# Idle products on a constant zero, a shorter table chain, an earlier load of one head's queries, one head's keys rounded on ScalarE, and the last two stores issued by ScalarE

## The chip, the cores and the metric

The kernel runs on one core of a Trainium2 chip. The metric is the device time of one execution in microseconds. Three runs of the kernel before took 411.08, 411.6 and 412.46 us; their median is 411.6 us. The engines are called by their short names: PE is TensorE (products), PEld its weight loads, DVE is VectorE, ACT is ScalarE, POOL is GpSimd and SP is SyncE, which here only issues transfers. A trailing q (SPq, ACTq, PEldq) means the sequencer that feeds the engine.

## The reference, cut to what matters

Three blocks in a row, all in float32. First an attention of 2 batches and 8 heads over 768 positions of 64 channels, in which each position sees the first `n_global` (8) positions and the last `n_local` (96), with a distance penalty for each head; then a block that rotates its input by learned angles and mixes it over positions and channels; then a gated block with a convolution over three positions.

```python
scores = scale * np.matmul(q, k.transpose(0, 1, 3, 2))
rel = pos[:, None] - pos[None, :]
is_global = pos[None, :] < int(n_global)
is_local = (rel >= 0) & (rel < int(n_local))
dist = np.where(is_global & ~is_local, float(n_local), np.abs(rel))
scores = scores - slopes[:, None, None] * dist[None, :, :]
scores = np.where(is_global | is_local, scores, -1e9)
a = softmax(scores); attn = np.matmul(a, v)
...
theta = x @ w_theta; zr, zi = x * np.cos(theta), x * np.sin(theta)
y = np.einsum('ts,bsd->btd', w_tok_r, zr) + np.einsum('ts,bsd->btd', w_tok_i, zi)
u = x + y; x = u + np.maximum(u @ w_ch, 0.0)
...
h = np.maximum(x @ w_in, 0.0)
out = (h * sigmoid(conv3(h, conv_w))) @ w_out
```

The large products are made of float32 numbers split into a rounded high part and the rest, three products for one, so that PE can run them in its faster rounded format.

## The kernel before, in words

`begin` runs ahead of everything. It loads the four words of `n_global` and `n_local` (L1036, on ACT's queue), the keys of heads 0 and 1 (`pairs`, L1038, on SP's queue) and the queries of head 0 (L1041, on ACT's queue). It lets PE make idle products whose results nobody reads (L1043 and L1044): they multiply `scratch[D:P]`, 64 partitions that DVE has just filled with zeros (L1042), by themselves. POOL writes the distances into `R` (L1051 to L1054). DVE turns the words into the floats `ng` and `nl` (L1063 to L1067), makes the flag `fi` that says whether the fast path holds (L1071 to L1073), and builds `table`, the masked distance of each of 232 columns, with a second form `X` of its last 128 columns for the first row of tiles (L1074 to L1079).

`build` then reads `fi` into a register of each engine (L1023) and branches (L1026). `arm` opens the pools of the fast path, and `run_fast` does the work. Its order is written out by hand: one loop over `j`, three steps for each of 16 heads (i = j // 3), and in a step the scores of step j, the softmax of j - 1 (DVE, L377), the exponentials of j - 2 (ACT, L386), the transposes of j - 3 (PE, L395), their copy out of PSUM for j - 4 (ACT, L82) and the product with V for j - 5 (PE). Each engine executes its instructions in this order, and the code of the steps sets it.

Heads 0 to 7 (`WHOLE`) use unrounded queries and keys, two heads to one tile of keys. A query of an even head fills the upper 64 partitions of its tile `whole[i % 4]` and the lower 64 are zero, an odd one the other way. `query` loads one (L329), `pair` two with their keys (L334). Heads 8 to 15 use split numbers: `load` brings queries (L254) and the keys' lower half (L255) into a stage by SP's queue, `keys` brings the keys a second time into the final tile by POOL's queue, which rounds them on the way (L260), and `split` makes the rest: ACT rounds the scaled queries (L304), DVE makes the queries' low part (L308) and the keys' low part (L90 with the form 64x816, input `qk`). Between these, `net.run` converts weights that arrive as 64 bit floats (L98 on ACT, L102, L106, L110 and L90 on DVE). From head 9 on, products `TH<-wth,xTs` of the second block are placed between those of the heads.

`tables` makes the scaled penalty of a head on POOL, for head 0 on DVE (L341). `Mix.tail` follows with the rest of the network, and `ff_out` ends it: each of 12 tiles of the output is copied from PSUM and stored by SP's queue (L700), the last tile in two halves, the first copied by ACT and the second by DVE. After the last store every engine branches to the end of the program, where SP waits for the transfers' semaphores and all engines meet.

Of the kernel before, what the change touches and what calls it, by code (L numbers as in the profile page):

```python
# [12 lines left out]
F32 = mybir.dt.float32  # L13
F32R = mybir.dt.float32r
I32 = mybir.dt.int32
AF = mybir.ActivationFunctionType
ALU = mybir.AluOpType
AX = mybir.AxisListType

B, H, S, D = 2, 8, 768, 64  # L20
DM, DFF = H * D, 1024
P = 128
NT = S // P
KC = DM // P
NF = DFF // P
NH = B * H
NG = 8
NPREV = 96
# [8 lines left out]
STAGE = S + NT * KW  # L37
BIG = float(2.0 ** 40)
# [2 lines left out]
TURN = 6.283185  # L41
TWO32 = float(2.0 ** 32)
WHOLE = range(8)
LAG_SM, LAG_EXP, LAG_T, LAG_EV, LAG_PV, LAG_N = 1, 2, 3, 4, 5, 6


REBIAS = 2.0 ** -112
QSCALE = -0.125


class Net:
# [173 lines left out]
class Attention:  # L225
# [21 lines left out]
    def load(self, i, whole=False):  # L247
        if whole or (i < NH and i not in WHOLE):
            b, h = divmod(i, H)
            src, st = self.net.io["qk"][b, :, h, :], self.st[i % 2]  # L250
            if whole:
                self.nc.sync.dma_start(st, src)
            else:
                self.nc.sync.dma_start(st[:, 0:S], src[:, 0:S])  # L254
                self.nc.sync.dma_start(st[D:P, S:STAGE], src[D:P, S:STAGE])  # L255

    def keys(self, i):
        if i < NH and i not in WHOLE:
            b, h = divmod(i, H)
            self.nc.gpsimd.dma_start(self.K(i), self.net.io["qk"][b, :, h, S:STAGE])  # L260

# [49 lines left out]
class FastAttention(Attention):  # L311
# [3 lines left out]
    def __init__(self, net, xs):  # L315
        super().__init__(net, xs)
        self.state = {}
        self.o = {}
        x, y = net.head["scratch"], xs[1].rearrange("p t d -> p (t d)")
        self.whole = [x[:, 0:S], y[:, 0:S], y[:, STAGE : STAGE + S], x[:, STAGE : STAGE + S]]  # L320
        self.both = [x[:, S:STAGE], y[:, S:STAGE]]

    def half(self, i):
# [12 lines left out]

    def tables(self, i):

        e = self.nc.gpsimd if i else self.nc.vector
        x = 2.0 ** -(i % H + 1) / (QSCALE if i in WHOLE else 1.0)  # L340
        e.tensor_scalar(self.bias[i % 2], self.net.head["table"], x, None, op0=ALU.mult)  # L341

    def chunks(self, tp):
        return [(u, a) for u in range(2) for a in range(2) if 2 * tp + u > 0 or a == 1]
# [4 lines left out]
    def scores(self, j):  # L349
# [4 lines left out]
        sp = net.bank("TH", 1) if tp == 2 and i < NH // 2 + 2 else net.bank("S", 2)  # L354
        if i in WHOLE:
            Q, K = self.whole[i % 4].unsqueeze(1), self.both[i // 2 % 2]
# [11 lines left out]
    def softmax(self, j):  # L368
        net, s = self.net, self.state[j]
        s["nm"] = net.small.tile([P, 2], F32, tag="nm", name=net.uid("nm"), bufs=3)  # L370
        i, tp = divmod(j, 3)
        bias = self.bias[i % 2].bitcast(F32)
        for u in range(2):
            c, t = slice(RW * u, RW * u + RW), bias[:, 0:RW]
            if tp + u == 0:
                c, t = slice(PG, RW), bias[:, RW:]
            self.nc.vector.tensor_tensor_reduce(  # L377
                self.sS[tp][:, c], s["sp"][:, c], t, scale=QSCALE if i in WHOLE else 1.0, scalar=3.0e38,
                op0=ALU.add, op1=ALU.min, accum_out=s["nm"][:, u : u + 1],
            )  # L380
# [84 lines left out]
class Mix:  # L465
# [223 lines left out]
    def ff_out(self, b, t, bank, e, c=slice(0, DM)):  # L689
        n = self.net  # L690
        k = 0
        for f in range(NF):
            g, w = self.g[b][f], self.wout[f]
            tc = slice(P * t, P * t + P)
            for a, x in ((0, 0), (1, 0), (0, 1)):
                n.mm(bank[:, c], g[:, a, tc], w[:, x, c], k == 0, k == 3 * NF - 1)
                k += 1
        o = n.tmp()
        n.hi(e, o[:, c], bank[:, c])
        self.nc.sync.dma_start(n.io["out"][b, P * t : P * t + P, c], o[:, c])  # L700

    def tail(self, early):

# [160 lines left out]
def run_fast(tc, net):  # L864
    nc, io = net.nc, net.io
    xs = [net.slot(f"xs{b}", [P, NT, DM], F32, "xs") for b in range(2)]
    att = FastAttention(net, xs)
    mix = Mix(net, xs)
    att.tables(0)
    att.query(1)  # L870
    nc.scalar.activation(att.whole[1][0:D], net.head["half_pi"][0:D].to_broadcast([D, S]), AF.Copy, scale=0.0)
    att.tables(1)
    nc.gpsimd.memset(att.whole[2][D:P], 0.0)
    att.load_v(0)
# [33 lines left out]
    for j in range(NJ + LAG_N + 3):  # L908
        i, tp = divmod(j, 3)
# [22 lines left out]
                att.keys(i + 2)  # L932
        if i > 0 and i + 1 not in WHOLE:
            if tp == 0:
                att.split(i + 1, "  A")
            elif tp == 1:
                att.split(i + 1, "   V")
                att.split(i + 1, " V")
# [15 lines left out]
        if splits and (splits[0][0] == 0 or theta0 == "done"):  # L954
            b, c = splits.popleft()
# [76 lines left out]
def begin(nc, io, net, small, head, idle):  # L1032

    w = small.tile([P, 4], I32, name="words")
    scratch = small.tile([P, 2584], F32, name="scratch")
    nc.scalar.dma_start(w, io["n"].bitcast(I32).rearrange("(o n) -> o n", o=1).to_broadcast([P, 4]))  # L1036
    for x in (slice(0, 2 * KW), slice(2 * KW, NT * KW)):
        nc.sync.dma_start(scratch[:, S:STAGE][:, x], io["pairs"][0, :, x])  # L1038
    qc = (slice(0, 2 * P), slice(2 * P, S))
    for x in qc:  # L1040
        nc.scalar.dma_start(scratch[0:D, x], io["qk"][0, 0:D, 0, x])  # L1041
    nc.vector.memset(scratch[D:P, 0:S], 0.0)  # L1042
    for x in (512, 512, 256):  # L1043
        net.mm(idle[:, 0:x], scratch[D:P, 0:P], scratch[D:P, 0:x], True, True)  # L1044
    nc.vector.memset(scratch[0:D, STAGE : STAGE + S], 0.0)

    R = scratch[:, STAGE + S : STAGE + S + RW]
    table = small.tile([P, RW + P], F32, name="table")
    T, X = table[:, 0:RW], table[:, RW:]
    V, G, O = slice(0, NPREV), slice(NPREV, PG), slice(PG, RW)  # L1050
    nc.gpsimd.iota(R[:, V], pattern=[[-1, NPREV]], base=NPREV, channel_multiplier=1, allow_small_or_imprecise_dtypes=True)  # L1051
    nc.gpsimd.iota(R[:, G], pattern=[[1, NG]], base=0, channel_multiplier=0, allow_small_or_imprecise_dtypes=True)
    nc.gpsimd.iota(R[:, O], pattern=[[-1, P]], base=0, channel_multiplier=1, allow_small_or_imprecise_dtypes=True)
    nc.gpsimd.affine_select(R[:, O], R[:, O], pattern=[[-1, P]], compare_op=ALU.is_ge, fill=BIG, base=0, channel_multiplier=1)  # L1054
    hp = small.tile([P, 2], F32, name="hp")
    nc.vector.memset(hp, math.pi / 2)
    nc.scalar.activation(hp[:, 1:2], hp[:, 0:1], AF.Exp)
# [2 lines left out]
    qk0 = small.tile([P, 2 * S + NT * KW], F32R, name="qk0")  # L1060

    f = small.tile([P, 8], F32, name="nf")
    nc.vector.tensor_copy(f[:, 0:4], w)  # L1063
    lo2, hi2 = f[:, 0:4:2], f[:, 1:4:2]
    nc.vector.tensor_scalar(f[:, 4:6], lo2, 0.0, None, op0=ALU.is_lt)
    nc.vector.tensor_tensor(f[:, 4:6], f[:, 4:6], hi2, op=ALU.add)
    nc.vector.scalar_tensor_tensor(f[:, 6:8], f[:, 4:6], TWO32, lo2, op0=ALU.mult, op1=ALU.add)  # L1067
    ng, nl = f[:, 6:7], f[:, 7:8]
    flag = small.tile([1, 2], F32, name="flag")
# [1 line left out]
    nc.vector.tensor_scalar(flag[:, 0:1], nl[0:1], 1.0, None, op0=ALU.is_ge)  # L1071
    nc.vector.scalar_tensor_tensor(flag[:, 1:2], nl[0:1], float(NPREV + 1), flag[:, 0:1], op0=ALU.is_le, op1=ALU.mult)
    nc.vector.scalar_tensor_tensor(fi, ng[0:1], float(NG), flag[:, 1:2], op0=ALU.is_le, op1=ALU.mult)  # L1073
    nc.vector.tensor_scalar(T, R, nl, BIG, op0=ALU.is_ge, op1=ALU.mult)  # L1074
    nc.vector.tensor_tensor(T, T, R, op=ALU.max)
    nc.gpsimd.tensor_copy(X, T[:, O])
    nc.vector.tensor_scalar(T[:, G], R[:, G], ng, BIG, op0=ALU.is_ge, op1=ALU.mult)
    nc.vector.tensor_scalar(T[:, G], T[:, G], nl, None, op0=ALU.max)
    nc.vector.tensor_tensor(X[:, 0:NG], X[:, 0:NG], T[:, G], op=ALU.min)  # L1079
    nnl = small.tile([P, 1], F32, name="nnl")  # L1080
    head.update(scratch=scratch, qk0=qk0, table=table, ident=ident, half_pi=hp[:, 0:1], ng=ng, nl=nl, nnl=nnl, flag=fi)

# [35 lines left out]
```

## Time and profile before

| what | value |
|---|---|
| median of three runs | 411.6 us |
| the profiled execution, its own time | 412.71 us |
| span of the profile, first to last instruction | 410.8 us |
| PE busy | 400.4 us (97%), 2382 instructions |
| DVE busy | 324.5 us (79%) |
| ACT busy | 221.4 us (54%) |
| POOL busy | 27.1 us (7%) |
| share of PE in the chain that ended last | 92% |
| share of DMA, DVE and ACT in that chain | 3%, 2%, 2% |

The span is 1.9 us shorter than the execution's own time; that much lies outside the first and the last instruction. The chain that ended last is followed back from the last instruction to what released each step. PE is in 92% of it, so nearly every microsecond counts in which PE waits or works slowly, and work on other engines counts where PE waits for it. A row of the timeline gives start, duration, engine, line, operation, result and inputs, shapes, the count, and in brackets how long the engine had been idle and what ended that.

### The profile page before, as it was taken

Reading aid. Unit: us, or ns where it says so; the run is one execution under the profiler, and the core shown is the slowest. Engines: PE = TensorE matmul, PEld = TensorE weight load, DVE = VectorE, ACT = ScalarE, POOL = GpSimd, SP = SyncE. Lnnn points to the kernel's source line nnn. Section 1 sums busy time; section 2 is a strip of 40 time slices with the busy share of each in tenths; the row PEclk is TensorE's granted clock in tenths of the full one; section 3 lists DMA queues with packets and bytes.
Section 4 is the critical chain, followed back from the end, with each engine's and each line's share of the span. In section 5 each row is a group of like instructions: output and inputs, shape, how many; then the busy total and the mean of one; then the engine's idle time right before and its main releaser. Section 6 shows DMA issues by size and latency. Waiting matters only on the chain.

```text
span 410.8 us, 6485 instructions
## 1 busy us (share of the span) xinstructions
PE 400.4 (97%) x2382; PEld 377.0 (92%) x2382; DVE 324.5 (79%) x715; ACT 221.4 (54%) x435; POOL 27.1 (7%) x35
## 2 busy tenths in 40 slices
PE   8999997999999999999999999999999999999994
PEld 5999996899998999999999999999999998888884
DVE  5588999999678869999899999999999999600000
ACT  3878996788696967425344346456654554200000
POOL 3222332121000000000000000000000000000000
PEclk9999999999999999999999999999999999999998
DMA  5969877974100231137366333220000000211011
GB/s 132 297 174 288 270 200 222 246 220 122 37 2 0 77 93 64 40 110 230 96 221 205 104 112 107 71 103 19 0 2 0 2 0 2 77 51 51 27 51 59
DMA packets 15799, 42.94 MB, mean 105 GB/s; under 512 B 2128, under 2 KB 2576, under 8 KB 15760
## 3 DMA queue, kind: packets, MB, share of 16 engines
q1 hardware_dynamic: 14304, 38.92, 31.0%
q0 software_dynamic: 1152, 3.34, 3.0%
q8 instruction: 20, 0.33, 0.3%
q10 hardware_dynamic: 304, 0.20, 0.2%
q14 instruction: 19, 0.16, 0.1%
HBM read 39.31 MB, written 3.15 MB: 103 GB/s over the span
## 4 chain that ended last, share of the span: by engine, by line
PE 92%; DMA 3%; DVE 2%; ACT 2%; issue 0%; DVEq 0%
PE O L93 24%; PE S L93 23%; PE PT L93 16%; PE TH L93 14%; PE X L93 9%; PE PT L395 4%; DMA qk<-qk 3%; PE idle L93 1%; PE X L519 1%; DVE qk L90 0%; ACT a L386 0%; ACT qk L304 0%; ACT a L82 0%; DVE a L377 0%; DVE xTs L90 0%
## 5 line engine op out<-in xcount | busy, mean ns | idle before, releaser
L386 ACT ACTIVATE a<-a,nm 128x232 f32<-128x232 f32 (+1 forms) x96 | 40.3, 471 | 12.5 <-DVE nm L377 12.4
L377 DVE CUSTOM_DVE_ANT_0 a<-S,qk 128x232 f32<-128x232 f32 (+1 forms) x76 | 25.3, 370 | 8.4 <-PE PT L395 6.1
L93 PE MATMUL O<-a,a 128*128 128x65 f32 x236 | 29.9, 268 | 0.0
L98 ACT ACTIVATE wbit<-wst 128x512 f32<-128x512 f32 (+1 forms) x38 | 23.3, 616 | 11.8 <-DMA wst<-w_ch 4.8
L93 PEld LDWEIGHTS O<-a,a 128*128 128x128 f32 x236 | 29.0, 192 | 0.2
L82 ACT ACTIVATE a<-PT 128x512 f32<-128x512 f32 (+1 forms) x48 | 26.6, 554 | 4.3 <-PE PT L395 4.2
L395 PE MATMUL PT<-ident,a 128*128 128x128 f32 x176 | 27.1, 273 | 0.0
L93 PE MATMUL O<-wt,z 128*128 128x384 f32 x144 | 26.9, 335 | 0.0
L93 PE MATMUL TH<-wth,xTs 128*128 128x512 f32 x96 | 26.2, 408 | 0.5 <-ACT scratch L563 0.5
L93 PE MATMUL PT<-wt,z 128*128 128x384 f32 x132 | 25.8, 335 | 0.0
L110 DVE SCALAR_TENSOR_TENSOR wbit<-wst,wbit 128x512 int32<-128x512 int32 (+1 forms) x38 | 24.6, 646 | 1.0
L93 PEld LDWEIGHTS O<-wt,z 128*128 128x128 f32 x144 | 25.2, 188 | 0.1
L106 DVE SCALAR_TENSOR_TENSOR wbit<-wst,wbit 128x512 int32<-128x512 int32 (+1 forms) x38 | 24.0, 631 | 0.9
L82 ACT ACTIVATE wt<-wbit 128x384 fp32r<-128x384 f32 x24 | 12.6, 527 | 21.9 <-DVE wbit L110 11.3
L102 DVE TENSOR_SCALAR wbit<-wbit 128x512 int32<-128x512 int32 (+1 forms) x48 | 19.0, 396 | 5.9 <-ACT wbit L98 5.7
L341 POOL TENSOR_SCALAR qk<-table 128x360 fp32r<-128x360 f32 x15 | 19.9, 1326 | 51.4 <-DVE nm L377 50.6
L93 PEld LDWEIGHTS PT<-wt,z 128*128 128x128 f32 x132 | 23.2, 188 | 0.0
L395 PEld LDWEIGHTS PT<-ident,a 128*128 128x128 f32 x176 | 20.8, 141 | 1.3
L93 PE MATMUL S<-wt,z 128*128 128x384 f32 x120 | 22.0, 336 | 0.0
L93 PEld LDWEIGHTS S<-wt,z 128*128 128x128 f32 x120 | 21.0, 188 | 0.0
L93 PEld LDWEIGHTS TH<-wth,xTs 128*128 128x128 f32 x96 | 17.0, 189 | 3.8 <-ACT scratch L563 0.7
L93 PE MATMUL O<-x,win 128*128 128x384 f32 x96 | 17.4, 337 | 0.0
(225 smaller groups left out, 944.7 us busy)
## 6 DMA issues: line engine op xcount, KB each, us to landing
wst<-w_tok SPq DMA_DIRECT2D x18, 384.0 KB, 3.7
a<-v SPq DMA_DIRECT2D x16, 357.5 KB, 5.5
wst<-w_out SPq DMA_DIRECT2D x8, 512.0 KB, 3.2
qk<-qk POOLq DMA_DIRECT2D x8, 408.0 KB, 6.1
a<-qk SPq DMA_DIRECT2D x8, 384.0 KB, 3.7
out<-scratch SPq DMA_DIRECT2D x11, 256.0 KB, 2.0
wst<-w_in SPq DMA_DIRECT2D x5, 512.0 KB, 4.3
scratch<-w_tok SPq DMA_DIRECT2D x6, 384.0 KB, 3.5
```

Source lines behind the costliest of these rows:

```text
L82: self.nc.scalar.activation(out, in_, AF.Copy)
L93: self.nc.tensor.matmul(out, l, r, start=start, stop=stop)
L98: self.nc.scalar.activation(t.bitcast(F32), w[:, 1 : w.shape[1] : 2].bitcast(F32), AF.Copy, scale=REBIAS)
L102: self.nc.vector.tensor_scalar(t, t, 3, None, op0=ALU.logical_shift_left)
L106: self.nc.vector.scalar_tensor_tensor(t, w[:, 0 : w.shape[1] : 2], 29, t, op0=ALU.logical_shift_right, op1=ALU.bitwise_or)
L110: self.nc.vector.scalar_tensor_tensor(t, w[:, 1 : w.shape[1] : 2], -(1 << 31), t, op0=ALU.bitwise_and, op1=ALU.bitwise_or)
L341: e.tensor_scalar(self.bias[i % 2], self.net.head["table"], x, None, op0=ALU.mult)
L377: self.nc.vector.tensor_tensor_reduce(self.sS[tp][:, c], s["sp"][:, c], t, scale=QSCALE if i in WHOLE else 1.0, scalar=3.0e38, op0=ALU.add ...
L386: self.nc.scalar.activation(sS[:, c], sS[:, c], AF.Exp, bias=s["nm"][:, u : u + 1], scale=-1.0)
L395: self.nc.tensor.transpose(pt[:, c], sS[:, self.columns(u, a)], net.head["ident"])
L519: self.nc.tensor.transpose(xb[:, P * jj : P * jj + P], self.xs[b][:, t, P * c : P * c + P], n.head["ident"])
```

## The change

- The idle products read a constant zero of 128 partitions that exists before the program's own first instruction, and no longer `scratch`. Their columns go from 512 + 512 + 256 to 512 + 512 + 512 + 128.
- The words are no longer copied into floats; one operation replaces two in the sum of their halves.
- The distances in `R` are stored with the sign and scale that head 0 needs (factor `FIRST`, which is -4), so head 0's softmax reads `table` itself, and DVE's `tables(0)` goes. The 8 global columns are computed by POOL into a new tile `far`, the copy of 128 columns into `X` moves from POOL to DVE, and two short operations on DVE put `far` in its places.
- The queries of head 1 are loaded in `begin`, ahead of the branch, as SP's third transfer. For that the order of the four query tiles changes, and the zero half that ACT writes behind the branch is that of head 3.
- Head 10 (`ROUND`) no longer gets its keys by POOL's rounding transfer. SP loads its whole stage in one transfer, and ACT rounds the keys from the stage ahead of its queries.
- The two halves of the last output tile are stored by ACT's queue.

```diff
+ROUND = (10,)
+FIRST = 0.5 / QSCALE
...
-            if whole:
+            if whole or i in ROUND:
                 self.nc.sync.dma_start(st, src)
             else:
                 self.nc.sync.dma_start(st[:, 0:S], src[:, 0:S])
                 self.nc.sync.dma_start(st[D:P, S:STAGE], src[D:P, S:STAGE])
     def keys(self, i):
-        if i < NH and i not in WHOLE:
+        if i < NH and i not in WHOLE and i not in ROUND:
...
-        self.whole = [x[:, 0:S], y[:, 0:S], y[:, STAGE : STAGE + S], x[:, STAGE : STAGE + S]]
+        self.whole = [x[:, 0:S], x[:, STAGE : STAGE + S], y[:, STAGE : STAGE + S], y[:, 0:S]]
...
-        e = self.nc.gpsimd if i else self.nc.vector
         x = 2.0 ** -(i % H + 1) / (QSCALE if i in WHOLE else 1.0)
-        e.tensor_scalar(self.bias[i % 2], self.net.head["table"], x, None, op0=ALU.mult)
+        self.nc.gpsimd.tensor_scalar(self.bias[i % 2], self.net.head["table"], x / FIRST, None, op0=ALU.mult)
...
-        bias = self.bias[i % 2].bitcast(F32)
+        bias = self.bias[i % 2].bitcast(F32) if i else net.head["table"]
...
-        self.nc.sync.dma_start(n.io["out"][b, P * t : P * t + P, c], o[:, c])
+        q = self.nc.scalar if (b, t) == (1, NT - 1) else self.nc.sync
+        q.dma_start(n.io["out"][b, P * t : P * t + P, c], o[:, c])
...
-    att.tables(0)
-    att.query(1)
-    nc.scalar.activation(att.whole[1][0:D], net.head["half_pi"][0:D].to_broadcast([D, S]), AF.Copy, scale=0.0)
+    nc.scalar.activation(att.whole[3][0:D], net.head["half_pi"][0:D].to_broadcast([D, S]), AF.Copy, scale=0.0)
...
-                att.split(i + 1, "  A")
+                att.split(i + 1, "A A" if i + 1 in ROUND else "  A")
...
+    nc.sync.dma_start(scratch[D:P, STAGE : STAGE + S], io["qk"][0, D:P, 1, 0:S])
...
-    for x in (512, 512, 256):
-        net.mm(idle[:, 0:x], scratch[D:P, 0:P], scratch[D:P, 0:x], True, True)
+    zero = nc.const_aps.tensor(0.0, [P, 512], F32)
+    for x in (512, 512, 512, 128):
+        net.mm(idle[:, 0:x], zero[:, 0:P], zero[:, 0:x], True, True)
...
-    nc.vector.tensor_copy(f[:, 0:4], w)
-    lo2, hi2 = f[:, 0:4:2], f[:, 1:4:2]
-    nc.vector.tensor_scalar(f[:, 4:6], lo2, 0.0, None, op0=ALU.is_lt)
-    nc.vector.tensor_tensor(f[:, 4:6], f[:, 4:6], hi2, op=ALU.add)
+    lo2, hi2 = w[:, 0:4:2], w[:, 1:4:2]
+    nc.vector.scalar_tensor_tensor(f[:, 4:6], lo2, 0.0, hi2, op0=ALU.is_lt, op1=ALU.add)
...
-    nc.vector.tensor_scalar(T, R, nl, BIG, op0=ALU.is_ge, op1=ALU.mult)
-    nc.vector.tensor_tensor(T, T, R, op=ALU.max)
-    nc.gpsimd.tensor_copy(X, T[:, O])
-    nc.vector.tensor_scalar(T[:, G], R[:, G], ng, BIG, op0=ALU.is_ge, op1=ALU.mult)
-    nc.vector.tensor_scalar(T[:, G], T[:, G], nl, None, op0=ALU.max)
-    nc.vector.tensor_tensor(X[:, 0:NG], X[:, 0:NG], T[:, G], op=ALU.min)
+    far = small.tile([P, NG], F32, name="far")
+    nc.gpsimd.tensor_scalar(far, R[:, G], ng, BIG, op0=ALU.is_ge, op1=ALU.mult)
+    nc.gpsimd.tensor_scalar(far, far, nl, FIRST, op0=ALU.max, op1=ALU.mult)
+    nc.vector.tensor_scalar(T, R, 1.0 / FIRST, nl, op0=ALU.mult, op1=ALU.is_ge)
+    nc.vector.scalar_tensor_tensor(T, T, FIRST * BIG, R, op0=ALU.mult, op1=ALU.min)
+    nc.vector.tensor_copy(X, T[:, O])
+    nc.vector.tensor_tensor(X[:, 0:NG], X[:, 0:NG], far, op=ALU.max)
+    nc.vector.tensor_copy(T[:, G], far)
```

The line numbers move by two in most of the file. At three places the order of an engine is needed further on.

PE at the start of the program before; `idle` are the idle products, `S_154`, `S_157` and `TH_163` the scores of head 0:

```order
L1018 UNCONDITIONAL_BRANCH
L93 MATMUL idle<-scratch 128x512 x2
L93 MATMUL idle<-scratch 128x256
L1023 TENSOR_LOAD fi
L1026 COMPARE_AND_BRANCH
L93 MATMUL S_154<-scratch 128x128
```

PE at the same place after the change:

```order
L1018 UNCONDITIONAL_BRANCH
L95 MATMUL idle<-const-float32-0.0 128x512 x3
L95 MATMUL idle<-const-float32-0.0 128x128
L1023 TENSOR_LOAD fi
L1026 COMPARE_AND_BRANCH
L95 MATMUL S_154<-scratch 128x128
```

The idle products no longer read what DVE writes, and there are 1664 columns of them instead of 1280.

DVE from the arrival of the words to its first softmax before; `nf` holds `ng` and `nl`:

```order
L1063 CAST nf<-words 128x4
L1065 TENSOR_SCALAR nf<-nf 128x2
L1066 TENSOR_TENSOR nf<-nf 128x2
L1067 SCALAR_TENSOR_TENSOR nf<-nf 128x2
...
L1073 SCALAR_TENSOR_TENSOR fi<-nf,flag 1x1
L1074 TENSOR_SCALAR table<-scratch,nf 128x232
L1075 TENSOR_TENSOR table<-table,scratch 128x232
L1077 TENSOR_SCALAR table<-scratch,nf 128x8
L1078 TENSOR_SCALAR table<-table,nf 128x8
L1079 TENSOR_TENSOR table<-table 128x8
...
L341 TENSOR_SCALAR qk_6_135<-table 128x360
```

The same stretch after the change:

```order
L1067 SCALAR_TENSOR_TENSOR nf<-words 128x2
L1068 SCALAR_TENSOR_TENSOR nf<-nf,words 128x2
L1072 TENSOR_SCALAR flag<-nf 1x1
L1073 SCALAR_TENSOR_TENSOR flag<-nf,flag 1x1
L1074 SCALAR_TENSOR_TENSOR fi<-nf,flag 1x1
L1078 TENSOR_SCALAR table<-scratch,nf 128x232
L1079 SCALAR_TENSOR_TENSOR table<-table,scratch 128x232
L1080 COPY table<-table 128x128
L1081 TENSOR_TENSOR table<-table,far 128x8
L1082 COPY table<-far 128x8
```

Two operations ahead of `fi` are gone, the table takes five operations as before, and nothing stands between the branch and the softmax.

ACT around the queries of head 10 before (`qk_91` is its tile, `a_3_132` its stage):

```order
L82 ACTIVATE a_5_134<-PT_727 128x512
L304 ACTIVATE qk_91<-a_3_132 128x768
L386 ACTIVATE a_5_134<-a_5_134,nm_750 128x232 x2
L82 ACTIVATE a_3_132<-PT_755 128x384
L386 ACTIVATE a_5_134<-a_5_134,nm_773 128x128
```

And after the change, where the tiles are numbered `qk_93` and `a_3_134`:

```order
L84 ACTIVATE a_5_136<-PT_726 128x512
L84 ACTIVATE qk_93<-a_3_134 128x816
L306 ACTIVATE qk_93<-a_3_134 128x768
L387 ACTIVATE a_5_136<-a_5_136,nm_748 128x232 x2
L84 ACTIVATE a_3_134<-PT_753 128x384
L387 ACTIVATE a_5_136<-a_5_136,nm_772 128x128
```

One rounding of 816 columns comes ahead of that of the queries; all else keeps its order.

## Rows read from the trace of the kernel before

**Rows 1.** The page, part 2: granted clock of PE in 40 slices, tenths

```profile
PEclk9999999999999999999999999999999999999998
```

**Rows 2.** The chain that ended last, 0 to 30 us: start, duration, what

```profile
0.96 0.71 DVE scratch L1042
...
1.71 4.64 PE idle L93 x6
...
6.49 3.09 PE S L93 x8
9.57 1.55 PE TH L93 x4
...
12.04 0.33 PE PT L395 x3
...
13.59 0.79 PE TH L93 x4
...
15.43 0.67 PE S L93 x4
```

**Rows 3.** Timeline of the start, DVE from the words to the first softmax

```profile
4.19 0.17 DVE L1063 CAST nf<-words 128x4 f32<-128x4 int32 x1 [1.61 <-DMA words<-n]
...
4.79 0.16 DVE L1067 SCALAR_TENSOR_TENSOR nf<-nf 128x2 f32<-128x2 f32 x1
...
5.34 0.15 DVE L1073 SCALAR_TENSOR_TENSOR fi<-nf,flag 1x1 int32<-1x1 f32 x1
5.42 0.32 DVE L1074 TENSOR_SCALAR table<-scratch,nf 128x232 f32<-128x232 f32 x1
...
6.93 0.17 DVE L1079 TENSOR_TENSOR table<-table 128x8 f32<-128x8 f32 x1
...
7.76 0.35 DVE L341 TENSOR_SCALAR qk<-table 128x360 fp32r<-128x360 f32 x1 [0.66 <-DVE table L1079]
...
8.26 0.29 DVE L377 CUSTOM_DVE_ANT_0 a<-S,qk 128x128 f32<-128x128 f32 x1 [0.15 <-DVE qk L341]
```

**Rows 4.** Line 1023, PE's sequencer: duration ns, first and last start

```profile
L1023 PEldq TENSOR_LOAD <-fi x1: 488/488/488, 5.5 to 5.5; - x1
```

**Rows 5.** Keys of heads 2 and 3: timeline, then issue to landing, us

```profile
7.88 0.58 SPq L334 DMA_DIRECT2D xs<-pairs  x1
...
xs<-pairs SPq DMA_DIRECT2D x1, 408.0 KB, 6.1
```

**Rows 6.** Timeline, 56 to 72 us, around heads 10 and 11

```profile
58.15 0.84 ACT L304 ACTIVATE qk<-a 128x768 fp32r<-128x768 f32 x1
...
61.45 0.58 POOL L260 DMA_DIRECT2D qk<-qk  x1 [0.83 <-PE PT L395]
62.30 1.00 DVE L90 TENSOR_TENSOR qk<-a,qk 64x816 fp32r<-64x816 f32 x1 [1.25 <-DMA qk<-qk]
...
63.36 0.71 PE L93 MATMUL S<-qk 128*128 128x128 f32 x4 [1.16 <-DVE qk L90]
...
64.25 0.87 ACT L386 ACTIVATE a<-a,nm 128x232 f32<-128x232 f32 x2 [2.51 <-DVE nm L377]
...
68.83 1.00 DVE L90 TENSOR_TENSOR qk<-a,qk 64x816 fp32r<-64x816 f32 x1
...
71.02 0.71 PE L93 MATMUL S<-qk 128*128 128x128 f32 x4 [0.67 <-DVE nm L377]
```

**Rows 7.** Issue to landing of POOL's transfer that starts at 61.45

```profile
qk<-qk POOLq DMA_DIRECT2D x1, 408.0 KB, 6.8
```

**Rows 8.** The last store, and the sequencers' last instructions, by line

```profile
406.01 0.33 SPq L700 DMA_DIRECT2D out<-scratch  x1
...
L1026 ACTq COMPARE_BRANCH  x1: 38/38/38, 402.6 to 402.6; - x1
...
L1018 SPq EVENT_SEMAPHORE  x14: 17/28/28, 409.2 to 410.8; - x14
...
L1018 ACTq DRAIN  x2: 8/44/80, 405.3 to 410.3; - x2
```

More of the change, by code (lines that the diff above doesn't have):

```diff
@@ L1050, in begin @@
     V, G, O = slice(0, NPREV), slice(NPREV, PG), slice(PG, RW)
[L1051 to L1054, printed above, removed]
+    iota = dict(allow_small_or_imprecise_dtypes=True)
+    nc.gpsimd.iota(R[:, V], pattern=[[4, NPREV]], base=-4 * NPREV, channel_multiplier=-4, **iota)
+    nc.gpsimd.iota(R[:, G], pattern=[[1, NG]], base=0, channel_multiplier=0, **iota)
+    nc.gpsimd.iota(R[:, O], pattern=[[4, P]], base=0, channel_multiplier=-4, **iota)
+    nc.gpsimd.affine_select(R[:, O], R[:, O], pattern=[[-1, P]], compare_op=ALU.is_ge, fill=FIRST * BIG, base=0, channel_multiplier=1)
     hp = small.tile([P, 2], F32, name="hp")
```

## The prediction

> **What bounds the kernel now.** I read the chain of waits first: PE products fill nearly all of it, so a gain must end a PE wait, raise PE's speed, or shorten the ends of the program. PE is weak in three places.
>
> The first is the start. PE begins at 1.71, released by DVE's fill of zeros; idle products take 4.64 us and the scores follow at 6.49 [rows 2]. The clock row shows full speed from the first slice [rows 1], but the durations contradict it: the same four score products of 232 columns take 1.55 us at 9.57 and 0.79 at 13.59 [rows 2]. That is the ratio of the two levels, 1.2 and 2.4 GHz, so PE runs at 1.2 GHz until about 11.7, between these rows. What precedes the rise: idle products on 64 partitions from 1.71, then 5.2 us of scores on 128 partitions from 6.49, with hardly a gap.
>
> The second is head 10. DVE waits 1.25 us at 62.30 for POOL's transfer of the keys, and PE 1.16 us at 63.36 behind it [rows 6]. The third is the end: the last store is issued at 406.01, yet the last instructions lie near 410.8 [rows 8].
>
> **The change, part by part.**
>
> *Branch.* Of the DVE steps between the words (4.19) and L1067 (4.79), three in 0.60 us, one of about 0.20 is left [rows 3]. So `fi`, written by 5.49, is there at 5.09. PE's register load starts at once and takes 0.49 [rows 4]; the scores begin 1.00 after `fi` [rows 2, 3]. The branch then allows scores from 6.09.
>
> *Idle products.* The constant exists before the program, so PE need not wait for DVE's fill; I let it start with DVE, at 0.96 [rows 2]. 1664 columns instead of 1280 cost 4.64 x 1664 / 1280 = 6.03 us at the lower level, ending at 7.0: alone this makes the scores later, 7.1 instead of 6.49. Everything hangs on when the clock rises. Bounds from rows: never earlier than before (11.7), or ahead of the first score. One rise can be carried over in two ways. Counted from the first product on 128 partitions it took 5.2 us, which from 0.96 gives 6.2. Counted from the first product at all, 1.71, it took about 9.9, which gives 10.9. I take 6.2, since the new products differ from the old in just this and follow each other without a gap. By 6.2, 5.24 of the 6.03 us are done; the other 0.79 take half, the idle products end at 6.6 and the scores begin at 6.7.
>
> The Trainium skill ("TensorE: Matmul & The Clock Gate", Part 1) says that the throttled state is the default and that activity releases it, and that the point of the rise varies from run to run. If any activity counts, the old idle products should have raised the clock as well as the new ones do; the trace shows 1.2 GHz long after them, so the page alone would lead to the rival of a late rise.
>
> *Scores to head 2.* Before, the first transposes start at 12.04, behind four steps of scores, and head 2's scores at 15.43, 3.39 us later [rows 2]. The four steps of scores from 6.49 to 12.04 cost 0.67 + 0.79 + 0.79 + 0.67 = 2.92 us at the higher level [rows 2]. So head 2 comes at 6.7 + 2.92 + 3.39 = 13.0 instead of 15.43, 2.4 us earlier.
>
> What could be late instead? DVE: the table steps begin 0.4 earlier, at 5.02; 0.32 each for the two wide ones (bound 0.4), 0.2 each for three small ones, which are below L1074 in size, end near 6.4. POOL's two 8-column steps run while DVE does its wide ones. The register load and branch cost 0.66 [rows 3], so the first softmax can start at 7.1, where it was 8.26, and the first scores are done only at about 7.4. Transfers: the second pair's keys are issued at 7.88 and land 6.1 later, at 13.98 [rows 5]. SP comes out of the branch 0.4 earlier and has one issue of 0.58 less ahead, which gives 13.0 with the same transfer time, less with head 1's 192 KB out of the way. That is a dead heat with PE's 13.0, and I take 2.3 off the 2.4. Moving head 1's queries ahead costs SP nothing: its register load waits for `fi` anyway. Later transfers keep more slack.
>
> *Head 10.* ACT does one rounding of 816 columns more, 0.89 us by the 0.84 of 768 columns, ahead of L304 at 58.15 [rows 6]. The keys are then rounded at 59.1, the queries at 59.9, and DVE can do its subtraction at 62.30 - 1.25 = 61.05. ACT's later steps shift by 0.9; it idles 2.51 us before 64.25 [rows 6], which covers that. The single stage transfer must wait for both of DVE's readers of the stage, but nobody needs it before 58. What is late next is head 11: its keys still come by POOL at 61.45, landing 6.8 later at 68.25 [rows 6, 7]. DVE reached them at 68.83 and would now at 67.58, so 0.67 of the 1.25 can come back, and PE waits for DVE again at 71.02 [rows 6]. With less traffic beside it the transfer may land sooner. Bounds 0.58 and 1.25; I take 0.9.
>
> *End.* SP issues the last store at 406.01 for 0.33 us, branches, and goes on only at 409.2; then come twelve semaphore steps and the meeting of the engines [rows 8]. ACT shows the same pause: branch at 402.6, next instruction at 405.3, 2.7 us [rows 8]. After the change SP has branched early and its steps run beside the last store; ACT issues at 406.01, branches at 406.4 (406.7 if it issues more slowly), and is through at 409.1 to 409.4, where SP was through at 409.95. Gain 0.5 to 0.8, at worst 0; I take 0.6.
>
> The Trainium skill ("Trainium Kernel Development and Optimization", Key Constraints) says that issuing transfers from several engines saves only the sequencer's issue time. By that this part would be worth at most the 0.33 us of one issue [rows 8]; the rows let me expect more, because what goes is SP's branch and semaphore steps behind the issue.
>
> *Sum.* 2.3 + 0.9 + 0.6 = 3.8 us. From the profiled execution's own 412.71 (span 410.8 and 1.9 around it) that gives 408.9. The median of the runs is 411.6, 1.1 below the profiled one; I take the gain off the median: 407.8 us. PE leads the chain from there to the end, so I let what is won early stay.
>
> **Rivals.**
>
> 1. *The clock rises late.* If work as such counts, the rise comes near 10.9 or stays at 11.7. The scores start at 7.1 and lose half of the time until the rise: 1.9 to 2.3 us. Head 2 then starts at 7.1 + 6.31 + 1.9 to 2.3 = 15.3 to 15.7 instead of 15.43. The start gives +0.1 to -0.3, head 10 and the end 1.5: 410.0 to 410.4 us. For it: the old idle products did not raise the clock. Against: they used half of the partitions.
> 2. *Transfers take back part.* The keys of the second pair land at 13.6 instead of 13.0, only the 0.4 of the branch earlier, because the queue is busy; POOL's keys for head 11 take their full 0.67; the end gives nothing. 1.8 + 0.6 + 0 = 2.4: 409.2 us. For it: the landing time of 6.1 us is mostly queueing. Against: 192 KB leave that queue.
> 3. *Slower: the clock falls back.* With PE ahead of its suppliers it could pause before head 2, where scores end and small transposes and products of 65 columns follow, and be set back to 1.2 GHz. Each microsecond there costs 0.5, so it decides when the lower level lasts over 7.6 us. A stretch of 12 us costs 6: 411.6 - 3.8 + 6 = 413.8 us. For it: these products are short. Against: the same products kept the clock up before.
> 4. *The idle products simply last longer,* and the clock rises as before: the upper end of the first rival, 410.4 us, within what cannot be told from no change.
>
> **How the numbers follow.** Forecast 407.8 us, chance 0.60, its own range 406.8 to 408.8. Rival 2: 0.18. Rivals 1 and 4 together: 0.17. Rival 3 and the like: 0.05. The moment of the rise can differ between runs and moves the start by some 0.5 us either way; the end and head 10 together by 0.6. The range goes from 406.3 to 410.1, which leaves out the upper part of rivals 1 and 4 and rival 3. About 0.3%, or 1.2 us, is what a measurement of this kernel can tell from no change: 410.4. Faster holds the forecast, rival 2 and over half of rivals 1 and 4: 0.88. Same 0.08, slower 0.04.
>
> **What would show it.** Right: the score products at 0.79 us for four from the first ones on; head 2's scores near 13.0; the first softmax near 7.5; PE's wait of 1.16 before head 10 gone, and DVE's subtraction for head 11 waiting a little for its transfer; ACT's and no longer SP's sequencer last at the end, with 4.1 us instead of 4.8 from the last store to the end. Wrong: scores of 1.55 us up to 11 us, a PE wait before head 2 for keys, or a new PE wait behind ACT near 60.

## The result and the profile after

The changed kernel takes 407.93 us (median of 19 runs, 407.4 to 410.6), the kernel before 412.41 (19 runs): a ratio of 0.9898, interval 0.9883 to 0.9913. The profiled execution of after took 407.4 us, its span is 405.5 us against 410.8. These 5.3 us are what the rows account for; by the medians the gain is 4.5, because this execution is at the quick end of its kernel's runs and that of before 0.3 above its median. A second set of six runs of after, further down, has a median of 409.18; over all 25 it is 408.08.

The start by the chain of waits of after (start, duration, what; it answers to [rows 2]):

```profile
6.46 1.64 PE S L95 x8
8.09 0.78 PE TH L95 x4
8.87 0.61 PE S L95 x4
9.49 0.33 PE PT L396 x3
...
12.88 0.67 PE S L95 x4
```

The scores start where they started before, 6.46 against 6.49. But eight take 1.64 us instead of 3.09, and the four of 232 columns 0.78 instead of 1.55: by these durations TensorE's clock is at 2.4 GHz from the first score on. (The rows of granted clock can't tell: the clock record of each trace begins only with the rise, and ahead of it they read 1.00 in both kernels.) The first transposes come at 9.49 instead of 12.04, and head 2's scores at 12.88 instead of 15.43: 2.55 us. That is the difference of these two executions. In the profile of e9 (below), whose start is that of before, the clock rises 1.8 us earlier and head 2 comes at 14.54.

The timeline of PE and DVE in after, from the idle products to the first softmax, answers to [rows 2, 3]:

```profile
0.78 5.42 PE L95 MATMUL idle<-const-float32-0.0 128*128 128x512 f32 x8 [0.78 <-PEq L1114]
...
4.55 0.16 DVE L1067 SCALAR_TENSOR_TENSOR nf<-words 128x2 f32<-128x2 int32 x1 [1.97 <-DMA words<-n]
...
5.32 0.15 DVE L1074 SCALAR_TENSOR_TENSOR fi<-nf,flag 1x1 int32<-1x1 f32 x1
...
7.46 0.29 DVE L378 CUSTOM_DVE_ANT_0 a<-S,table 128x128 f32<-128x128 f32 x1 [0.69 <-PE S L95]
```

The idle products took 5.42 us; with the clock at the lower level to their end the same columns take 5.88 (e2 below). Work done at the higher level takes half the time, so the 0.46 saved stand for 0.46 us at that level ahead of the end at 6.20: by this estimate the clock rose near 5.7. The clock record of the trace has the rise at 5.58, and in before at 11.64. DVE's chain from the words to `fi` is 0.92 long instead of 1.30, but it starts 0.36 later (4.55, was 4.19): the words landed later. `fi` stands at 5.47, where it was at 5.49.

The keys of the second pair, which [rows 5] gave 6.1 us, in the list of transfers of after:

```profile
xs<-pairs SPq DMA_DIRECT2D x1, 408.0 KB, 4.9
```

They were issued at 7.01 and landed near 11.9, a microsecond before PE needed them.

The timeline around heads 10 and 11 in after answers to [rows 6]:

```profile
58.54 1.01 DVE L92 TENSOR_TENSOR qk<-a,qk 64x816 fp32r<-64x816 f32 x1
58.90 0.58 POOL L262 DMA_DIRECT2D qk<-qk  x1 [0.82 <-PE PT L396]
59.60 0.72 PE L95 MATMUL S<-qk 128*128 128x128 f32 x4
...
65.08 1.01 DVE L92 TENSOR_TENSOR qk<-a,qk 64x816 fp32r<-64x816 f32 x1
...
67.17 0.71 PE L95 MATMUL S<-qk 128*128 128x128 f32 x4 [0.57 <-DVE nm L378]
68.04 1.00 PE L95 MATMUL O<-a,a 128*128 128x65 f32 x8
```

Neither DVE nor PE waits at head 10: its scores come at 59.60 instead of 63.36, 3.76 earlier, 1.21 more than at head 2. POOL's transfer for head 11, issued at 58.90, took 5.9 us (6.8 in [rows 7]) and landed at 64.8, just ahead of DVE's subtraction at 65.08, so nothing was given back; head 11's scores are 3.85 earlier.

The end answers to [rows 8]; first the timeline of after, then the sequencers' last instructions by line:

```profile
401.50 0.34 ACTq L702 DMA_DIRECT2D out<-scratch  x1
```

```profile
L1026 ACTq COMPARE_BRANCH  x2: 38/43/48, 6.0 to 401.9; - x2
...
L1018 SPq EVENT_SEMAPHORE  x13: 17/28/28, 399.3 to 405.5; - x13
...
L1018 ACTq DRAIN  x2: 8/44/80, 404.6 to 405.0; - x2
```

The last store is issued 4.51 us earlier, so 0.66 more were won between head 11 and here. From the store to the end of the span it is 4.0 us instead of 4.8: SP begins its semaphore steps at 399.3, two microseconds before the last store, and ACT arrives 2.7 us behind its branch (401.9, 404.6), later than SP. The account: 2.55 (start), 1.21 and 0.09 (heads 10 and 11), 0.66 (between), 0.8 (end), together 5.3 us.

### The profile page after: what moved, and what is told of

It is laid out like the page before. It is cut to its first block, busy times and chain, and to the rows that moved or that the text cites. A ratio compares the mean times of both kernels' runs of the same rounds, so it can differ in the third digit from the quotient of the medians.

```text
span 405.5 us, 6477 instructions
## 1 busy us (share of the span) xinstructions
PE 398.0 (98%) x2384; PEld 375.5 (93%) x2384; DVE 323.5 (80%) x712; ACT 222.2 (55%) x436; POOL 27.0 (7%) x35
## 4 chain that ended last, share of the span: by engine, by line
PE 89%; DVE 7%; DMA 1%; issue 1%; ACT 1%; DVEq 0%
PE O L95 24%; PE S L95 22%; PE PT L95 16%; PE TH L95 14%; PE X L95 9%; PE PT L396 3%; DVE a L378 2%; DVE qk L92 1%; DVE qk L310 1%; DMA words<-n 1%; PE X L520 1%; DVE xTs L92 1%; DVE xTs L88 0%; DVE wbit L112 0%; DVE wbit L108 0%
## 5 line engine op out<-in xcount | busy, mean ns | idle before, releaser
L378 DVE CUSTOM_DVE_ANT_0 a<-S,qk 128x232 f32<-128x232 f32 (+1 forms) x72 | 23.9, 370 | 7.2 <-PE PT L396 5.7
```

The lines of the kernel that those rows point to most:

```text
L378: self.nc.vector.tensor_tensor_reduce(self.sS[tp][:, c], s["sp"][:, c], t, scale=QSCALE if i in WHOLE else 1.0, scalar=3.0e38, op0=ALU.add ...
```

## The experiments

"From after" and "from before" name the kernel that was edited. Ratios are to runs of the kernel before on the same chip, with their 95% intervals.

**e1_idle_only**, from before: the new idle products alone.

```diff
-    for x in (512, 512, 256):
-        net.mm(idle[:, 0:x], scratch[D:P, 0:P], scratch[D:P, 0:x], True, True)
+    zero = nc.const_aps.tensor(0.0, [P, 512], F32)
+    for x in (512, 512, 512, 128):
+        net.mm(idle[:, 0:x], zero[:, 0:P], zero[:, 0:x], True, True)
```

> The kernel before with nothing changed but the idle products (constant zero of 128 partitions, 1664 columns). My theory (the new idle products raise the clock before the first scores): the four score products at 9.57 in the profile before take 0.79 us instead of 1.55 from the first ones on, head 2's scores move from 15.43 to about 13.0, and the time falls by 2.0 to 2.6 us; head 10's wait and the end stay as before. One extra risk: head 1's queries and head 2's keys are still loaded behind the branch, so head 2 may wait for keys that land near 14.0, and then the gain is 1.4 us. Rival (the earlier branch and the early load of queries do the work at the start): less than 0.5 us.

Measured 411.47 us (10 runs), ratio 0.9983, 0.9964 to 1.0001: 0.7 us by the medians, a miss, and not clear of no change. Its timeline of PE:

```profile
0.77 5.88 PE L93 MATMUL idle<-const-float32-0.0 128*128 128x512 f32 x8 [0.77 <-PEq L1112]
6.76 1.64 PE L93 MATMUL S<-scratch 128*128 128x128 f32 x8
...
13.75 0.46 PE L93 MATMUL S<-xs 128*128 128x128 f32 x2 [0.22 <-DVE nm L377]
...
62.13 0.72 PE L93 MATMUL S<-qk 128*128 128x128 f32 x4 [1.43 <-DVE qk L90]
63.02 1.00 PE L93 MATMUL O<-a,a 128*128 128x65 f32 x8
...
66.39 1.77 PE L93 MATMUL O<-a 128*128 128x65 f32 x8
```

The start's theory holds: the first eight scores take 1.64, and head 2 is 1.7 earlier. But at head 10 PE waits 1.43, more than before, and behind that the clock falls: the eight products of 65 columns take 1.77 us at 66.39 where the same shape took 1.00 at 63.02. The rows of granted clock by stretch (start:end, length, busy time and count of PE, PEld, DVE, ACT, POOL, then the clock):

```profile
64.00:66.00 2.00, 1.76 (x11) 1.74 (x11) 2.00 (x7) 2.00 (x5) 0.52 (x1) 0.64 1.00 249
66.00:68.00 2.00, 2.00 (x12) 2.00 (x11) 1.97 (x7) 2.00 (x6) 1.15 (x1) 0.50 0.04 14
68.00:70.00 2.00, 2.00 (x20) 2.00 (x21) 1.90 (x9) 1.31 (x4) 0.58 (x1) 1.00 0.68 181
```

What is won at the start is partly lost here: the clock at 0.50 is the level of 1.2 GHz.

**e2_half_rows**, from after: the same idle products on 64 partitions.

```diff
-        net.mm(idle[:, 0:x], zero[:, 0:P], zero[:, 0:x], True, True)
+        net.mm(idle[:, 0:x], zero[D:P, 0:P], zero[D:P, 0:x], True, True)
```

> The changed kernel with its idle products on 64 of the 128 partitions of the same constant; start, columns and order as in the change. Theory (what counts is that the idle products use all partitions): the clock rises only 4 to 6 us after the first scores, as in the kernel before, and the time is 2.0 to 2.8 us above the changed kernel, near 410.3. Rival (the earlier start, the greater length or the missing gap count): the clock rises before the first scores, and the time is that of the changed kernel, near 407.9.

Measured 409.92 us (10 runs), ratio 0.9956, 0.9937 to 0.9976: 2.0 above after. Its chain of waits:

```profile
0.77 5.88 PE idle L95 x8
6.76 3.08 PE S L95 x8
...
14.68 0.67 PE S L95 x4
```

The first eight scores run at the lower level for 3.08 us, and head 2 comes at 14.68. Start, columns and data are after's; the 64 partitions alone cost 1.8 us here. It isn't the chance of one execution: in all four profiles with idle products on 64 partitions (before, e2, e8, e9) these eight take 3.08 or 3.09, in all ten with 128 partitions 1.64.

**e6_late_full**, from after: 1280 columns as before, behind a fill by DVE, on 128 partitions.

```diff
-    zero = nc.const_aps.tensor(0.0, [P, 512], F32)
-    for x in (512, 512, 512, 128):
-        net.mm(idle[:, 0:x], zero[:, 0:P], zero[:, 0:x], True, True)
+    zero = small.tile([P, 1], F32, name="zero")
+    nc.vector.memset(zero, 0.0)
+    for x in (512, 512, 256):
+        net.mm(idle[:, 0:x], zero.to_broadcast([P, P]), zero.to_broadcast([P, x]), True, True)
```

> The changed kernel with 1280 idle columns as before, released by DVE at about 1.7 as before, but on 128 partitions. Theory (all partitions are what counts, 3 to 6 us after the first such product): the clock rises between 4.7 and 7.7, and the time is within 0.6 us of the changed kernel. Rival (the earlier start or the greater length counts): the clock rises near 10 or later, as with half the partitions, and the time is near 410.

Measured 408.5 us (4 runs, 407.12 to 408.86), ratio 0.9931, 0.9911 to 0.9951: 0.6 above after, which four runs can't tell from it. Its chain of waits:

```profile
6.27 1.64 PE S L95 x8
...
12.69 0.67 PE S L95 x4
```

With the old start and the old length the first scores are quick. Neither the constant nor the earlier or longer run of idle products is needed here, only the 128 partitions.

**e5_query_behind**, from after: head 1's queries issued behind the branch again.

```diff
+    att.query(1)
...
-    nc.sync.dma_start(scratch[D:P, STAGE : STAGE + S], io["qk"][0, D:P, 1, 0:S])
```

> The changed kernel with head 1's queries loaded as SP's first transfer behind the branch again. Theory (that transfer, ahead of the branch, shares the transfer engines with the four words and makes them land 3.8 us after their issue instead of 3.4): the words land at 4.1, the flag is 0.4 us earlier, the scores start near 6.2 instead of 6.46; but V and head 2's keys land 0.6 us or more later, head 2's scores wait for keys until about 13.5, and the time is 0 to 0.6 us above the changed kernel. Rival (the words' landing time varies by itself): the words land between 4.0 and 4.6 as in the other runs, and head 2 is still late.

Measured 408.61 us (10 runs, 408.1 to 413.62), ratio 0.9937, 0.9904 to 0.9969. Its timeline:

```profile
4.02 0.16 DVE L1067 SCALAR_TENSOR_TENSOR nf<-words 128x2 f32<-128x2 int32 x1 [1.44 <-DMA words<-n]
...
0.78 4.77 PE L95 MATMUL idle<-const-float32-0.0 128*128 128x512 f32 x8 [0.78 <-PEq L1114]
5.93 1.64 PE L95 MATMUL S<-scratch 128*128 128x128 f32 x8 [0.38 <-DVE table L1080]
...
8.94 0.85 PE L95 MATMUL S<-scratch 128*128 128x128 f32 x4 [0.59 <-DMA scratch<-qk]
...
68.88 1.01 PE L95 MATMUL S<-qk 128*128 128x128 f32 x4 [1.59 <-DVE nm L378]
...
70.32 1.81 PE L95 MATMUL O<-a,a 128*128 128x65 f32 x8
```

The words are there 0.53 earlier than in after and the scores start at 5.93, but head 1's wait 0.59 for their queries, and head 2 is 0.5 late. In this execution, of 412.84 us, POOL's transfer for head 11 took 7.2 us, PE waited 1.59 for the softmax behind it, and the clock fell: 1.81 for eight products of 65 columns.

**e7_old_table**, from after: the words and the table as before (the steps of the words and of the table, and `tables` on DVE for head 0; the tile `far` goes too).

```diff
-    nc.vector.scalar_tensor_tensor(f[:, 4:6], lo2, 0.0, hi2, op0=ALU.is_lt, op1=ALU.add)
+    nc.vector.tensor_copy(f[:, 0:4], w)
...
-    far = small.tile([P, NG], F32, name="far")
...
+    att.tables(0)
```

> The changed kernel with the old words, table and first-table chain. Theory (the chain sets DVE's first softmax, and PE at the higher level now waits for it): first softmax 0.8 to 1.2 us later, the first transposes wait for the exponentials, head 2's scores 0.3 to 0.8 us later, and the time 0.3 to 0.8 us above the changed kernel. Rival (PE has enough scores to make meanwhile): no difference behind head 2's first scores.

Measured 409.08 us (10 runs), ratio 0.9942, 0.9921 to 0.9963, 1.1 above after. Scores start at 6.64 and head 2's at 13.36, 0.48 later than in after. Its last stage is 0.65 longer as well, as in every kernel here without the tile `far` or one like it (e9). POOL's transfer for head 11 took 7.2 us in this execution; two rows of its timeline are needed at the end:

```profile
68.73 0.71 PE L95 MATMUL S<-qk 128*128 128x128 f32 x4 [1.64 <-DVE nm L379]
...
69.60 1.00 PE L95 MATMUL O<-a,a 128*128 128x65 f32 x8
```

**e8_round_only**, from before: head 10's keys rounded by ACT, and nothing else.

```diff
+ROUND = (10,)
...
-            if whole:
+            if whole or i in ROUND:
...
-        if i < NH and i not in WHOLE:
+        if i < NH and i not in WHOLE and i not in ROUND:
...
-                att.split(i + 1, "  A")
+                att.split(i + 1, "A A" if i + 1 in ROUND else "  A")
```

> The kernel before with head 10's keys rounded by ACT and nothing else. Theory: DVE's and PE's wait before head 10 goes, head 11's transfer is in time, and from head 11 on PE is 1.2 us earlier than in the kernel before: near 411.0. Rival (POOL's transfer for head 11 lands late and gives 0.67 back): 0.5 us earlier, near 411.7.

Measured 411.7 us (10 runs), ratio 1.0001, 0.9981 to 1.002. Its timeline:

```profile
61.02 1.01 DVE L91 TENSOR_TENSOR qk<-a,qk 64x816 fp32r<-64x816 f32 x1
62.09 0.71 PE L94 MATMUL S<-qk 128*128 128x128 f32 x4
...
68.16 1.01 DVE L91 TENSOR_TENSOR qk<-a,qk 64x816 fp32r<-64x816 f32 x1 [0.64 <-DMA qk<-qk]
...
70.25 0.71 PE L94 MATMUL S<-qk 128*128 128x128 f32 x4 [1.17 <-DVE nm L378]
```

Head 10 is 1.27 earlier. Then DVE waits 0.64 for head 11's keys and PE 1.17 instead of 0.67, so 0.77 is left at head 11 (70.25 against 71.02). By the medians 0.5 of it is left (412.2 for before on this chip), by the ratio nothing. Two of the ten runs, at 413.4 and 413.46, have a mean granted clock of 0.989, which takes part of it back.

**e3_no_round**, from after: `ROUND = ()`, all else kept.

```diff
-ROUND = (10,)
+ROUND = ()
```

> The changed kernel with head 10's keys by POOL's rounding transfer again, as before. Theory: DVE waits about 1.2 us for that transfer again, PE about as long, and from head 11 on PE is 1.2 to 1.3 us later than in the changed kernel: near 409.2. Rival (head 10's wait went because everything is 2.5 us earlier, or the wait would be made up by head 12): within 0.4 us of the changed kernel.

Measured 408.61 us (4 runs), ratio 0.9924, 0.9896 to 0.9952. The timeline of DVE and PE:

```profile
59.35 1.01 DVE L92 TENSOR_TENSOR qk<-a,qk 64x816 fp32r<-64x816 f32 x1 [1.15 <-DMA qk<-qk]
...
60.41 0.71 PE L95 MATMUL S<-qk 128*128 128x128 f32 x4 [1.06 <-DVE qk L92]
```

The wait is back, and head 10's scores are 0.81 later than in after, although this execution was 0.29 ahead at head 2 (12.59): the wait is worth 1.10. By the medians it is 0.7, within what four runs can't tell.

**e4_sp_stores**, from after: the last stores by SP.

```diff
-        q = self.nc.scalar if (b, t) == (1, NT - 1) else self.nc.sync
+        q = self.nc.sync
```

> The changed kernel with the last two stores on SP's queue as before. Theory (SP's branch and semaphore steps behind the last store are what was saved): from the last store's issue to the end of the span 4.8 us as before, 4.0 in the changed kernel, so 0.8 us slower, near 408.7. Rival (only the time of one issue is saved): 0.33 us or less slower.

Measured 408.04 us (4 runs), ratio 0.9914, 0.9884 to 0.9945: no difference that the times tell. Its timeline, and SP's sequencer at the end:

```profile
401.41 0.33 SPq L702 DMA_DIRECT2D out<-scratch  x1
```

```profile
L1018 SPq EVENT_SEMAPHORE  x13: 17/28/28, 404.4 to 405.9; - x13
```

The span ends at 406.0, 4.58 us behind the store, in after 4.02. The trace's price of this edit is 0.56 us: less than the 0.8 between before and after, more than SP's 0.33 of issue. The other 0.2 is the pause between SP's branch and its next instruction, 2.8 us in before (406.4, 409.2) and 2.6 here (401.8, 404.4). By the Trainium skill ("Trainium Kernel Development and Optimization", Key Constraints), issuing from several engines saves the issue time alone; the trace goes beyond that, since SP's semaphore steps start at 404.4 here and at 399.3 in after, while the last issue takes 0.33 or 0.34 us on either queue.

**f1_round_two** and **f2_round_three**, from after: heads 10 and 11, or 10 to 12, rounded by ACT. **after_again** is after once more, with these on one chip.

```diff
-ROUND = (10,)
+ROUND = (10, 11)        # f1
+ROUND = (10, 11, 12)    # f2
```

> The changed kernel with the keys of heads 10 and 11 rounded by ACT. Theory (POOL's rounding transfer lands 5.3 to 7.2 us after its issue, and head 11 waits for it whenever it takes over 6.1): the wait of up to 1.1 us of DVE and 1.6 us of PE before head 11 can no longer occur, a transfer of 408 KB goes, the slowest runs of the changed kernel near 410.5 disappear, and the median falls by 0 to 0.6 us, to 407.3 to 407.9. Rival 1 (head 12's transfer is late instead, by the same mechanism): no gain. Rival 2 (ACT, which has 0.87 us more in 7 us, sets the pace): 0.3 to 0.9 us slower.

> The changed kernel with the keys of heads 10, 11 and 12 rounded by ACT. Theory: head 12 has 6 products of the second block between its steps, so PE waits for nothing there and this gives nothing beyond heads 10 and 11: 407.3 to 407.9. Rival (head 12's transfer is late too): another 0.3 us faster than with heads 10 and 11.

> The changed kernel once more, on the same chip as the two above, to compare with: 407.9 us median, most runs between 407.4 and 408.6, one in ten near 410.5, in which the clock of PE is lower for a while because a wait near 67 us set it back; in this profile either POOL's transfer for head 11 lands within 6.1 us and PE waits about 0.6 us at head 11, or it lands later and PE waits over 1 us.

Measured: f1 408.4 us (6 runs), ratio 0.9889, 0.9868 to 0.991; f2 407.72 (5 runs), 0.9881, 0.9863 to 0.99; after 409.18 (6 runs), 0.9909, 0.9882 to 0.9937. The intervals overlap, so a better version is not shown. So the gain that was expected of f1 isn't shown either. Three of the six runs of after lay at 410.0 to 410.6, where one in ten was expected; the profile is of one (410.29), its timeline:

```profile
65.77 1.00 DVE L92 TENSOR_TENSOR qk<-a,qk 64x816 fp32r<-64x816 f32 x1 [0.94 <-DMA qk<-qk]
...
67.85 0.71 PE L95 MATMUL S<-qk 128*128 128x128 f32 x4 [1.47 <-DVE nm L378]
...
68.73 1.81 PE L95 MATMUL O<-a,a 128*128 128x65 f32 x8
```

and by stretch:

```profile
68.00:70.00 2.00, 2.00 (x14) 2.00 (x14) 1.97 (x8) 2.00 (x6) 0.04 (x1) 0.68 1.04 292
70.00:75.00 5.00, 5.00 (x22) 4.81 (x22) 4.94 (x11) 2.88 (x8) 1.23 (x1) 0.50 0.76 191
75.00:80.00 5.00, 5.00 (x34) 4.44 (x34) 3.78 (x15) 3.03 (x6) 1.52 (x2) 0.95 0.86 236
```

Here POOL's transfer took 7.1 us instead of 5.9. DVE waits 0.94, PE 1.47 instead of 0.57, and until about 75.5 the clock is at the lower level: eight products that took 1.00 in the first profile of after take 1.81. PE's wait is 0.9 longer; this execution was 0.21 ahead at head 10, so head 11's scores are 0.7 later (67.85 against 67.17). The clock costs some 2 us more: the time is 2.4 above after's median. The profiles of f1 and f2 show no such fall. A late transfer comes with a later head instead (DVE waits 1.30 us at 73.29 in f1, 0.82 at 90.67 in f2), and PE waits 1.32 near 65 behind ACT, which has more to round.

**e9_pad**, from before: an unused tile of 32 bytes a partition where after has `far`.

```diff
+    pad = small.tile([P, NG], F32, name="pad")
+    nc.gpsimd.memset(pad, 0.0)
```

> The kernel before with one more tile of 8 columns (32 bytes of each partition) beside the table, which POOL fills with zeros and nobody reads; it stands where the change has its tile of 8 columns, and moves the tiles allocated behind it as that one does. Theory (the place of the tiles in memory makes the last products quicker in the changed kernel): the products of the last stage that read the weights in qk take 390 ns in the profile instead of 396, the others 389 instead of 391, the last 312 products 65.8 us instead of 66.45, and the time falls by about 0.65 us, which the timed runs may not tell from nothing. Rival (something else of the new table chain does it): 396 and 391 ns as in the kernel before.

Measured 411.61 us (10 runs), ratio 0.9979, 0.9964 to 0.9995. One group of its last stage (busy us, mean ns):

```profile
L93 PE MATMUL O<-qk,g 128*128 128x512 f32 x24 | 6.1, 390 | 0.0
```

The same group of before, and of after:

```profile
L93 PE MATMUL O<-qk,g 128*128 128x512 f32 x24 | 6.2, 396 | 0.0
```

```profile
L95 PE MATMUL O<-qk,g 128*128 128x512 f32 x24 | 6.1, 390 | 0.0
```

From the first of these products to the end of the last it is 66.45 us in before, 65.80 in after and 65.80 here. All profiles fall into these two: 66.45 in the four without a tile in this place (before, e1, e7, e8), 65.80 in the others. An unused tile, which does nothing in this stage but take its place in memory ahead of what is allocated behind it, is worth 0.65 us: the 0.66 between head 11 and the last store. Which tile's place does it, and how, is open; `qk` itself is allocated ahead of it in the program.

## Why the prediction came true, step by step

The forecast was 407.8 us, the median is 407.93. It is nearer than its working deserves: the gain came out at 4.5 instead of 3.8, from 412.4 where the runs shown had 411.6, and that the two differences cancel is luck.

- *Branch, 0.4.* The chain is shorter by 0.38, as worked out; the words are later by 0.36. "Moving head 1's queries ahead costs SP nothing" looked at SP alone. DVE's first step on the words starts at 4.24 to 4.55 in the nine profiles with head 1's queries ahead of the branch and at 4.01 to 4.19 in the five without (means 4.36 and 4.07): the queries hold the words up by about 0.3. In the traces they stay worth it, since e5 loses more to its wait for them (head 2 is 0.49 later); by the times that isn't clear.
- *Idle products, the clock at 6.2.* It rose at 5.58. By the clock records of the other traces it rose at 4.26 in e5 and only at 6.54 in e1, where the idle products end at 6.65: the spread is wider than I gave it. The first scores are at the higher level all the same, since the branch does not let them begin earlier. That the partitions decide, which I took from the difference between the old and the new products, is shown by e2 against after and by e6. The Trainium skill ("TensorE: Matmul & The Clock Gate", Part 1) says that activity releases the clock; in e2 idle products on 64 partitions ran for 5.9 us and the scores behind them were still at the lower level.
- *Head 2 at 13.0.* 12.88, with 2.55 instead of 2.3 for the start. The dead heat with the keys was won by a microsecond, because the transfer took 4.9 instead of the 6.1 I kept.
- *Head 10, 0.9 between 0.58 and 1.25.* 1.21, the upper end, where POOL's transfer takes 5.9 us. In after_again it takes 7.1, and PE's wait at head 11 is 0.9 longer; 0.67 was the most that I let come back. The profile of after shows the better case: of the eight profiles in which head 10 alone is rounded by ACT, four have a transfer of 5.3 to 6.0 us and a wait of 0.56 or 0.57, four one of 6.8 to 7.2 and a wait of 1.17 to 1.64.
- *End, 0.6.* 0.8 in the trace, of which e4 gives 0.56 to the issuing engine; by the times e4 differs from after by 0.1, which four runs can't tell from nothing.
- *Not in the sum.* The 0.65 of the last stage. No edit of the change aims at it; I did not ask what a new small tile moves.

The rivals: 1 and 4 (a late rise, 410.0 to 410.4) did not happen, but e2, which makes the rise late (9.81), measures 409.92: the price was about right. Rival 2 happens in part, in some runs. Rival 3's mechanism is real and was put in the wrong place: not before head 2, but behind late keys, of head 11 in two profiles and of head 10 in e1. In the kernels that round head 10 alone, 13 of 73 runs have a mean granted clock of 0.991 or less, in the other experiments and the runs of before beside them none of 103; a profile was taken of two of the 13, and both show the fall near 69 us. The count finds long falls only: e1's of 3.4 us leaves that run's mean at 0.995.

Put into before one at a time, the parts do not add up. The idle products alone gave 0.7 us and the rounding alone 0.5 or nothing; within the whole the start gave 2.55 and head 10 1.21 in the trace. A start that is quicker alone runs into the wait at head 10 and into the clock behind it (e1); a rounding alone leaves PE slow at the start and gives 0.5 to the next transfer (e8). Taken out of after one at a time, they do, by the medians: 2.0 for the partitions (e2), 1.1 for the table (e7, with the 0.65 of the last stage in it), 0.7 for the rounding (e3), 0.7 for head 1's queries (e5) and 0.1 for the stores (e4) are 4.6 us. Only the first two are clear of noise, so the agreement may be chance.

Open: why POOL's transfer of the same 408 KB takes 5.9 us in one run and 7.1 in another; and why the clock falls behind some waits and not behind others. The three falls stand behind the longest waits of PE in their profiles, 1.43, 1.47 and 1.59 us, and the profiles whose waits are 1.32 or less show none; but e7 waited 1.64 us at the same place and its products of 65 columns stayed at 1.00. So that the wait sets the clock back is likely, and not shown.

## What to carry to other kernels

Warm-up products should look like the work that follows them: here products on 64 partitions did not bring the clock up in time and those on 128 did, all else the same. Where a wait of PE is removed, look at the next transfer of the same queue and at what the clock does behind a wait of a microsecond and a half, since a fall costs more than the wait did (some 2 us against 0.9 in after_again). A transfer that is moved ahead of a branch competes with whatever the branch waits for.

## What the runs showed of the hardware that was not expected

- An unused tile of 32 bytes a partition changed the mean of 128x512 products with `qk` as the moving operand from 396 to 390 ns, and their stage from 66.45 to 65.80 us (e9).
- TensorE's clock fell to 1.2 GHz in the middle of the kernel, behind a wait of 1.43 to 1.59 us among short products, for 3.4 us (e1), 7 us (after_again) and 10 us (e5), and rose again while PE worked on. A wait of 1.64 us in e7 had no such fall behind it.
- Idle products on 128 partitions that began at the same 0.77 to 0.78 were at the higher level from 4.26 (e5), 5.58 (after) or 6.54 us on (e1), by the clock records of the traces: the rise is not a fixed distance from the first product.
- Idle products on 64 partitions from 0.77 to 6.65 us left the clock at 1.2 GHz until 9.81, on 128 partitions it was at 2.4 GHz in all ten profiles before the first score (e2, after).
